# The feed-forward's operands turned by DMA transposes in a fused FNet and GEGLU kernel

## The chip, the cores and the metric

The kernel runs on one core of a Trainium2 chip. The metric is the device time in microseconds of one execution. The core has five engines that work in parallel, each through its own queue in program order: PE (TensorE, matmuls), DVE (VectorE), ACT (ScalarE), POOL (GpSimd) and SP (SyncE), which here issues every DMA. They wait for one another by semaphores. The data moves on 16 DMA engines.

## The reference

One transformer layer on x of shape 2048 x 448: h = x + FNet(layernorm(x)), then out = h + GEGLU(layernorm(h)).

```python
a = einsum("bsd,ed->bse", x, dft_hid_re);  b = einsum("bsd,ed->bse", x, dft_hid_im)
y = einsum("ts,bse->bte", dft_seq_re, a) - einsum("ts,bse->bte", dft_seq_im, b)
h = x + y                                   # x in the two lines above is layernorm(x)
g = einsum("bsd,df->bsf", n, w_gate);  u = einsum("bsd,df->bsf", n, w_up)   # n = layernorm(h)
out = h + einsum("bsf,fd->bsd", gelu(g) * u, w_down)
```

The width of the feed-forward is 1792.

## The kernel before

All matmuls take float16 operands. To keep float32 accuracy every operand is split into a high part (`hi_part`, a copy on ACT, L103) and a low part (`lo_part`, the difference, on DVE, L107 or L109), and a product is three matmuls (high x high, high x low, low x high).

The kernel has two stages. The order of the work is written out by hand: every engine runs its queue in the order in which the program names the instructions, and two tables, `early` and `after`, and later `side`, hang extra pieces of work on numbered steps.

**Stage 1, the Fourier mixing** (to about 368 us): 64 steps, `n` = 0 to 63, 16 for each block `b` of 512 outputs. Step n loads two tiles of the sequence matrix ahead (`seq_load`, SP, L366, five buffers), splits them three steps ahead (ACT L103, DVE L109) and runs 18 matmuls of 512 columns (L414) and, now and then, the remainder (L428). After a block the hidden transform follows in four pieces (`hid_mm`, L479), one every other step of the next block, and h comes out. Beside it, in steps of three, one of 14 feed-forward weight tiles is loaded, split and stored to DRAM (`Weights`; the store is L335). The blocks of h are kept in DRAM too (L490).

**Stage 2, the feed-forward** (from about 368 us): 56 steps `t`, 14 for each of four blocks `q`. Gate and up products use a Strassen scheme: a step takes 39 matmuls of 256 columns (`product`, L718) on the weight tile `gw` (loaded back by SP, L798, three buffers) and on the block's operands `hops`; from q = 1 on it takes 21 matmuls of the down projection (L662) as well.

**The operands `hops`.** A block q has two pairs j of 2 x 128 tokens (`hp[q, j]`). For each pair the kernel normalises h (`ffn_norm`, or `ffn_norm_act` for q = 2 and 3), forms the Strassen sums (`ffn_sums`), and splits them into one float16 tile `xs` of 128 tokens x 3200 columns (`ffn_hi`, `ffn_lo`). PE needs these operands with the 448 features on the partitions, so `ffn_transpose` turns the 25 column blocks of 128 of `xs` into the 25 slots of `hops[q]`, in four parts of 8, 8, 6 and 3 blocks. Each part is one tile `pt` in a single PSUM bank (`ps_tr`, tag "tr", which the pieces of `hid_mm` use as well): 8 matmuls against the identity on PE (L285), then one copy PSUM to SBUF on ACT (L287).

For q = 0 and 1 that happens in stage 1: pair j of block b splits at step n + 5 and transposes at steps n + 6, n + 7 and twice n + 9, with n = 16 (b + 1) + 1 + 6 j. For q = 2 and 3 it happens in stage 2, two blocks of steps ahead of their use: with t0 = 14 (q - 1) + 6 j the split ends in step t0 + 5, and the parts are transposed in steps t0 + 4, t0 + 5 and twice t0 + 6. `xs` has one buffer, `hops` has two.

Of the kernel before, what the change touches and what calls it, by code (L numbers as in the profile page):

```python
# [8 lines left out]
F16 = mybir.dt.float16  # L9
F32 = mybir.dt.float32  # L10
AF = mybir.ActivationFunctionType
ALU = mybir.AluOpType

P = 128
# [18 lines left out]
def kernel(  # L33
# [35 lines left out]
    nc = tc.nc  # L69
    V, A, G, PE = nc.vector, nc.scalar, nc.gpsimd, nc.tensor  # L70
# [7 lines left out]
    ps_tr = ctx.enter_context(tc.tile_pool(name="ps_tr", bufs=1, space=bass.MemoryType.PSUM))  # L78
# [3 lines left out]
    ident = const.tile([P, P], F16, name="ident")  # L82
# [195 lines left out]
    def ffn_transpose(q, j, parts):  # L278
        xs = ffn[q, j][2]
        ops = hops[q]  # L280
        for n in parts:
            s0, s1 = ((0, 8), (8, 16), (16, 22), (22, 25))[n]
            pt = ps_tr.tile([P, 8, P], F16, tag="tr", name=f"pt_{q}_{j}_{n}")
            for k in range(s0, s1):
                PE.transpose(pt[:, k - s0, :], xs[:, k * P : (k + 1) * P], ident)  # L285
            dst = ops[:, s0:s1, j * P : (j + 1) * P]
            A.activation(dst, pt[:, : s1 - s0], AF.Copy)  # L287


    for q in range(2):  # L290
# [47 lines left out]
    xt, xs, norm_x = {}, {}, {}  # L338
# [166 lines left out]
    for k, f in enumerate(reversed(range(NF))):  # L505
        n = 17 + 3 * k
# [4 lines left out]
    for b in range(NB):  # L511
        for j in range(2):
            n = (b + 1) * NT + 1 + 6 * j
            at(early, min(n - 4, N_STEPS - 3), lambda b=b, j=j: h_tile(b, j))
            if b == NB - 1:
                continue
            for g in range(2):
                at(after, (n + 2 * g, 0), lambda b=b, i=2 * j + g: hid_mm(b, i, ps_tr, "tr"))
            at(early, n + 3, lambda b=b, j=j: ffn_stats(b, j, hp[b, j]))
            at(early, n + 3, lambda b=b, j=j: h_store(b, j))  # L520
            if b < 2:
                at(early, n + 3, lambda b=b, j=j: ffn_norm(b, j, hp[b, j]))
                at(early, n + 4, lambda b=b, j=j: ffn_sums(b, j))
                at(early, n + 5, lambda b=b, j=j: ffn_split(b, j))
                for k, when in enumerate(((n + 6, 1), (n + 7, 1), (n + 9, 0), (n + 9, 1))):
                    at(after, when, lambda b=b, j=j, k=k: ffn_transpose(b, j, (k,)))
# [388 lines left out]
    for q in (2, 3):  # L915
        for j in range(2):
            t0 = (q - 1) * NF + 6 * j
            for f, k, what in (
                (0, 1, lambda q=q, j=j: ffn_norm_act(q, j, hp[q, j])),
                (1, 1, lambda q=q, j=j: ffn_sums(q, j, (0,))),  # L920
                (1, 2, lambda q=q, j=j: ffn_sums(q, j, (1,))),
                (2, 1, lambda q=q, j=j: ffn_sums(q, j, (2,))),
                (2, 1, lambda q=q, j=j: ffn_hi(q, j, (0,))),
                (2, 2, lambda q=q, j=j: ffn_sums(q, j, (3,))),
                (2, 2, lambda q=q, j=j: ffn_lo(q, j, (0,))),
                (3, 1, lambda q=q, j=j: ffn_hi(q, j, (1,))),
                (3, 2, lambda q=q, j=j: ffn_lo(q, j, (1,))),
                (4, 1, lambda q=q, j=j: ffn_lo(q, j, (2,))),
                (4, 2, lambda q=q, j=j: ffn_lo(q, j, (3,))),
                (5, 1, lambda q=q, j=j: ffn_lo(q, j, (4,))),  # L930
                (4, 4, lambda q=q, j=j: ffn_transpose(q, j, (0,))),
                (5, 4, lambda q=q, j=j: ffn_transpose(q, j, (1,))),
                (6, 4, lambda q=q, j=j: ffn_transpose(q, j, (2,))),
                (6, 5, lambda q=q, j=j: ffn_transpose(q, j, (3,))),
            ):
                at(side, (t0 + f, k), what)

    for t in range(3 * NF, N_GU):
        f = t % NF
        if f < NF - 1:  # L940
            n, k = divmod(f, 2)
# [28 lines left out]
    for t in range(N_GU):  # L970
        q, f = divmod(t, NF)
# [58 lines left out]
    for i in range(4):  # L1030
        j, g = divmod(i, 2)
# [68 lines left out]
```

## Time and profile before

| | |
|---|---|
| median of 3 runs | 741.58 us (741.35 to 742.21) |
| the profiled execution | 741.01 us, span of its instructions 738.9 us |
| granted TensorE clock | 1.00 throughout |
| busy: PE, DVE, ACT, POOL | 731.1, 500.8, 295.2, 234.1 us |
| DMA transposes | none |
| L285, 200 TensorE transposes | 16.4 us busy on PE |
| L287, 32 copies from PSUM | 26.7 us busy on ACT |
| DMA on SP's queue | 132.43 MB in 36832 packets, 51.1% of 16 engines |

A row of a group reads: line, engine, operation, output <- input, shapes, count | busy us, mean ns of one | idle us of that engine just before, and what ended it. A row of a timeline reads: start us, length us, engine, line, operation, output <- input, count, and in brackets an idle time before it. SPq is SP's queue. "us to landing" of a DMA is the time from its issue to its data being there.

### The profile page before, as it was taken

The page shows a single profiled execution, that of the slowest core. Times are in us where ns is not written, and L with a number is a line of the kernel's source. Part 1 is how long each engine was busy: PE and PEld are TensorE (multiplying, and loading weights), DVE is VectorE, ACT ScalarE, POOL GpSimd, SP SyncE. Part 2 cuts the span into 40 slices and gives each one's busy share as a digit, 9 for nine tenths or more (in the row PEclk, how much of TensorE's full clock was granted, in tenths as well). Part 3 has the DMA queues.
Part 4 walks back from the last instruction along what each step waited for, and adds up shares of the span by engine and source line. Part 5 has one row for each costly group of instructions (what it writes and reads, how often), then busy time and mean ns, then how long its engine had stood idle before and what let it go on. Part 6 is the DMA issues. An engine that isn't in the chain of part 4 may idle for free.

```text
span 738.9 us, 13783 instructions
## 1 busy us (share of the span) xinstructions
PE 731.1 (99%) x5530; PEld 511.3 (69%) x5530; DVE 500.8 (68%) x1026; ACT 295.2 (40%) x567; POOL 234.1 (32%) x274
## 2 busy tenths in 40 slices
PE   9999999999999999999999999999999999999998
PEld 5444444444444444444488889999999999999998
DVE  7888665577655776450477778687786977988730
ACT  4444613348223572221143354544545444454310
POOL 0000000000000001000058865477674866858430
PEclk9999999999999999999999999999999999999999
DMA  8666464474645567621057654345535446465411
GB/s 275 227 215 236 157 228 177 141 266 178 228 178 204 203 226 281 260 81 45 26 182 279 239 198 170 117 166 175 174 118 194 155 161 226 170 229 201 150 39 38
DMA packets 36896, 133.31 MB, mean 180 GB/s; under 512 B 3680, under 2 KB 12896, under 8 KB 36832
## 3 DMA queue, kind: packets, MB, share of 16 engines
q1 hardware_dynamic: 36832, 132.43, 51.1%
q8 instruction: 43, 0.70, 0.4%
q14 instruction: 21, 0.17, 0.1%
HBM read 112.23 MB, written 20.19 MB: 179 GB/s over the span
## 4 chain that ended last, share of the span: by engine, by line
PE 93%; DVE 3%; DMA 2%; ACT 2%; issue 0%; SPq 0%; DVEq 0%
PE acc L414 32%; PE pY L718 13%; PE acc_d L662 11%; PE y L479 9%; PE pX L718 8%; PE pZ L718 8%; PE acc L428 6%; PE pt L285 1%; PE last_Y L881 1%; PE last_X L881 1%; PE last_tr L881 1%; DMA x<-in_x_dram 1%; DMA gw<-w_dram 1%; DVE dn_w L107 1%; PE last_a L881 1%; PE last_Z L881 1%
## 5 line engine op out<-in xcount | busy, mean ns | idle before, releaser
L414 PE MATMUL acc<-ws,xs 128*128 128x512 f16 x1152 | 256.2, 379 | 0.2 <-DVE xs L107 0.2
L718 PEld LDWEIGHTS <-gw 128*128 128x128 f16 x2067 | 201.2, 98 | 23.9 <-issue 2.4
L414 PEld LDWEIGHTS <-xs 128*128 128x128 f16 x1152 | 110.6, 98 | 135.4 <-issue 6.1
L718 PE MATMUL pY<-hops,gw 128*128 128x256 f16 x901 | 123.0, 273 | 1.9 <-DVE u L728 1.7
L109 DVE SCALAR_TENSOR_TENSOR ws<-wr,ws 128x1024 f16<-128x1024 f32 (+1 forms) x66 | 78.0, 1188 | 44.1 <-ACT ws L103 44.1
L662 PE MATMUL acc_d<-wd,dn_w 128*128 128x224 f16 x882 | 105.1, 259 | 0.0
L201 POOL TENSOR_TENSOR wd_s<-wd 128x448 f32<-128x448 f32 x7 | 7.9, 1131 | 281.2 <-DMA wd<-in_w_down_dram 281.2
L662 PEld LDWEIGHTS <-dn_w 128*128 128x128 f16 x882 | 85.0, 98 | 2.9
L718 PE MATMUL pX<-hops,gw 128*128 128x256 f16 x583 | 81.0, 273 | 0.5 <-DMA gw<-w_dram 0.5
L718 PE MATMUL pZ<-hops,gw 128*128 128x256 f16 x583 | 79.2, 273 | 0.0
L785 POOL TENSOR_TENSOR hh<-hh,g 128x256 f32<-128x256 f32 x42 | 30.9, 736 | 146.1 <-DVE hh L728 127.6
L103 ACT ACTIVATE ws<-wr 128x1024 f16<-128x1024 f32 (+1 forms) x66 | 66.4, 1018 | 23.2 <-DMA wr<-in_w_seq_dram 13.3
L728 DVE SCALAR_TENSOR_TENSOR u<-pY,u 128x256 f32<-128x256 f32 x112 | 46.9, 419 | 29.5 <-ACT c L792 18.8
L479 PE MATMUL y<-wh,z 128*128 128x448 f16 x336 | 65.7, 352 | 0.0
L479 PEld LDWEIGHTS <-z 128*128 128x128 f16 x336 | 32.8, 98 | 31.6 <-issue 0.4
L107 DVE TENSOR_TENSOR dn_w<-dn_s,dn_w 128x640 f16<-128x640 f32 x42 | 53.2, 1266 | 1.4 <-ACT dn_w L103 0.9
L287 ACT ACTIVATE hops<-pt 128x1024 f16<-128x1024 f16 (+2 forms) x32 | 26.7, 834 | 67.3 <-PE pt L285 67.3
L487 DVE SCALAR_TENSOR_TENSOR hx<-y,hx 128x448 f32<-128x448 f32 x16 | 10.0, 624 | 62.4 <-PE y L479 62.4
L769 ACT ACTIVATE g<-pX 128x256 f32<-128x256 f32 x56 | 21.4, 381 | 73.3 <-PE pX L718 68.1
L756 ACT ACTIVATE u<-pX 128x256 f32<-128x256 f32 x56 | 21.4, 383 | 72.8 <-PE pX L718 72.7
L794 POOL TENSOR_TENSOR hh<-hh,c 128x256 f32<-128x256 f32 x42 | 40.9, 975 | 20.0 <-ACT c L792 20.0
L428 PE MATMUL acc<-ws,xs 128*64 128x512 f16 x384 | 44.7, 381 | 0.0
(110 smaller groups left out, 880.3 us busy)
## 6 DMA issues: line engine op xcount, KB each, us to landing
gw<-w_dram SPq DMA_DIRECT2D x53, 896.0 KB, 4.6
wr<-in_w_seq_dram SPq DMA_DIRECT2D x62, 512.0 KB, 6.2
w_dram<-gu_w SPq DMA_DIRECT2D x14, 896.0 KB, 4.7
gu_raw<-in_w_gu_dram SPq DMA_DIRECT2D x28, 384.0 KB, 5.6
wd<-in_w_down_dram SPq DMA_DIRECT2D x14, 448.0 KB, 5.3
x<-in_x_dram SPq DMA_DIRECT2D x16, 224.0 KB, 3.5
hx<-in_x_dram SPq DMA_DIRECT2D x8, 448.0 KB, 6.6
h_dram<-hx SPq DMA_DIRECT2D x8, 448.0 KB, 4.1
```

Source lines behind the costliest of these rows:

```text
L103: A.activation(dst, src, AF.Copy, scale=scale)
L107: V.tensor_sub(dst, src, hi)
L109: V.scalar_tensor_tensor(dst, src, scale, hi, op0=ALU.mult, op1=ALU.subtract)
L414: PE.matmul(acc[b, 3 * part + k], xs[c][:, lx, k * P : (k + 1) * P], seq_w(n, lw, part), start=c == 0 and m == 0, stop=c == NT - 1 and m == 2,
L428: PE.matmul(acc[b, 6][64 * part : 64 * part + 64, :], xs[c][:, lx, 3 * P :], seq_w(n, lw, part), start=c == 0 and m == 0, stop=c == NT - 1 ...
L479: PE.matmul(y[:, :D], z[b][:, lz, k, i * P : (i + 1) * P], wh[:, lw, k, :], start=k == 0 and m == 0, stop=k == 6 and m == 2,)
L662: PE.matmul(acc[k // 2][:, k % 2 * HD : (k % 2 + 1) * HD], a_of(la, a), b_of(lb, b), start=first and m == 0 and k % 2 == 0, stop=last and ...
L718: PE.matmul(ps, w[:, wl, wa + ws, :], ops[:, m + ms, :], start=first and n == 0, stop=last and n == len(terms) - 1, skip_group_check=True,)
L728: V.scalar_tensor_tensor(dst, ps, SC, other, op0=ALU.mult, op1=ALU.add)
L785: G.tensor_mul(c21, c21, self.g1)
L794: G.tensor_mul(c22, c22, self.c12)
L881: PE.matmul(banks[0][:, c * HD : (c + 1) * HD] if one else banks[c][:, 0:HD], last["h"][:, lh, f, tok], w, start=f == 0 and m == 0 and c = ...
```

## The change

In `ffn_transpose` the matmuls against the identity, the PSUM tile and the copy are replaced by one DMA per part, issued by SP, that reads the columns of `xs` and writes them transposed into the same slots of `hops`. Nothing else changes; the lines behind it move up by four.

```diff
         for n in parts:
             s0, s1 = ((0, 8), (8, 16), (16, 22), (22, 25))[n]
-            pt = ps_tr.tile([P, 8, P], F16, tag="tr", name=f"pt_{q}_{j}_{n}")
-            for k in range(s0, s1):
-                PE.transpose(pt[:, k - s0, :], xs[:, k * P : (k + 1) * P], ident)
-            dst = ops[:, s0:s1, j * P : (j + 1) * P]
-            A.activation(dst, pt[:, : s1 - s0], AF.Copy)
+            nc.sync.dma_start_transpose(ops[:, s0:s1, j * P : (j + 1) * P], xs[:, s0 * P : s1 * P])
```

SP's order in stage 1, around the first pair of block 0 (`wr` a tile of the sequence matrix, `gu_raw` and `w_dram` the feed-forward weights on their way in and out). Before:

```order
L366 DMA wr_1294<-in_w_seq_dram 128x1024
L366 DMA wr_1379<-in_w_seq_dram 128x1024
L366 DMA wr_1416<-in_w_seq_dram 128x1024
L335 DMA w_dram_165<-gu_w_1383 128x3584
L302 DMA gu_raw_1426<-in_w_gu_dram 128x768 x2
L366 DMA wr_1470<-in_w_seq_dram 128x1024
L490 DMA h_dram_147<-hx_1_1105 128x896
L366 DMA wr_1529<-in_w_seq_dram 128x1024
```

Now:

```order
L362 DMA wr_1294<-in_w_seq_dram 128x1024
L283 DMA_TRANSPOSE hops_168<-xs_0_1265 128x8x128
L362 DMA wr_1370<-in_w_seq_dram 128x1024
L283 DMA_TRANSPOSE hops_168<-xs_0_1265 128x8x128
L362 DMA wr_1398<-in_w_seq_dram 128x1024
L331 DMA w_dram_165<-gu_w_1374 128x3584
L298 DMA gu_raw_1408<-in_w_gu_dram 128x768 x2
L362 DMA wr_1452<-in_w_seq_dram 128x1024
L486 DMA h_dram_147<-hx_1_1105 128x896
L283 DMA_TRANSPOSE hops_168<-xs_0_1265 128x6x128
L283 DMA_TRANSPOSE hops_168<-xs_0_1265 128x3x128
L362 DMA wr_1500<-in_w_seq_dram 128x1024
```

The four parts stand between the weight loads, two of them in the row of three loads that had nothing between them.

SP's order in stage 2, around the second pair of block 2 (`gw` the weight tile of a step, `out_dram` a finished pair of outputs). Before:

```order
L798 DMA gw_5302<-w_dram_166 128x3584
L846 DMA out_dram<-hr_4411 128x2x448
L798 DMA gw_5406<-w_dram_167 128x3584
L798 DMA gw_5507<-w_dram_154 128x3584
L798 DMA gw_5609<-w_dram_155 128x3584
```

Now:

```order
L794 DMA gw_5157<-w_dram_166 128x3584
L283 DMA_TRANSPOSE hops_4194<-xs_1_5021 128x8x128
L842 DMA out_dram<-hr_4295 128x2x448
L794 DMA gw_5252<-w_dram_167 128x3584
L283 DMA_TRANSPOSE hops_4194<-xs_1_5021 128x8x128
L794 DMA gw_5344<-w_dram_154 128x3584
L283 DMA_TRANSPOSE hops_4194<-xs_1_5021 128x6x128
L283 DMA_TRANSPOSE hops_4194<-xs_1_5021 128x3x128
L794 DMA gw_5435<-w_dram_155 128x3584
```

Each weight load now has one or two transposes ahead of it.

ACT's order in stage 1, from the split of the first pair of block 0 on (`ws` the split of a sequence tile). Before:

```order
L103 ACTIVATE xs_0_1265<-tt_0_1228 128x192
L103 ACTIVATE ws_1296<-wr_1218 128x1024
L287 ACTIVATE hops_168<-pt_0_0_1345 128x8x128
L103 ACTIVATE ws_1296<-wr_1253 128x1024
L103 ACTIVATE gu_w_1383<-gu_raw_1102 128x512
L103 ACTIVATE gu_w_1383<-gu_raw_1102 128x256
L287 ACTIVATE hops_168<-pt_0_1_1406 128x8x128
L103 ACTIVATE ws_1418<-wr_1294 128x1024
```

Now:

```order
L103 ACTIVATE xs_0_1265<-tt_0_1228 128x192
L103 ACTIVATE ws_1296<-wr_1218 128x1024
L103 ACTIVATE ws_1296<-wr_1253 128x1024
L103 ACTIVATE gu_w_1374<-gu_raw_1102 128x512
L103 ACTIVATE gu_w_1374<-gu_raw_1102 128x256
L103 ACTIVATE ws_1400<-wr_1294 128x1024
```

The copies out of PSUM, which waited for PE, no longer stand between the splits. On PE the 8, 8, 6 and 3 transposes of a pair are taken out of the matmuls around them, whose order stays.

## The prediction

> **What bounds the kernel now.** I read the page's busy shares and its chain of waits first, then the table of stretches, then the PE timeline around the transposes.
>
> ```profile
> span 738.9 us, 13783 instructions
> PE 731.1 (99%) x5530; PEld 511.3 (69%) x5530; DVE 500.8 (68%) x1026; ACT 295.2 (40%) x567; POOL 234.1 (32%) x274
> PEclk9999999999999999999999999999999999999999
> PE 93%; DVE 3%; DMA 2%; ACT 2%; issue 0%; SPq 0%; DVEq 0%
> ...
> 0.00:60.00 60.00, 58.42 (x320) 28.68 (x320) 50.09 (x136) 27.43 (x46) 0.87 (x9) 1.00 0.71 233
> 60.00:368.00 308.00, 308.00 (x1695) 145.57 (x1695) 180.52 (x353) 115.03 (x181) 2.84 (x3) 1.00 0.52 184
> 368.00:445.00 77.00, 74.64 (x673) 65.41 (x671) 56.81 (x114) 33.36 (x71) 52.92 (x56) 1.00 0.64 222
> 445.00:704.00 259.00, 258.23 (x2517) 240.15 (x2516) 207.65 (x415) 118.37 (x269) 171.16 (x197) 1.00 0.49 170
> ```
>
> The first four rows are of the page. The others are the table of stretches: after the length come PE, PEld, DVE, ACT and POOL busy, then the granted clock and the share of the 16 DMA engines. The transposes lie in the second and the fourth stretch. There PE is busy 308.00 of 308.00 us and 258.23 of 259.00 us at full clock, and the chain of waits is 93% PE. DVE is the next engine, with 180.52 us (59%) and 207.65 us (80%). So in both stretches the time is what PE has in its queue, and a slot that leaves PE's queue leaves the span, as long as the data that took its way is there in time. ACT, at 37% and 46%, is not on the path.
>
> **What the change removes.** 200 TensorE transposes and 32 ScalarE copies:
>
> ```profile
> L285 PE MATMUL pt<-ident,xs 128*128 128x128 f16 x200 | 16.4, 219 | 0.8 <-ACT hops L287 0.8
> L287 ACT ACTIVATE hops<-pt 128x1024 f16<-128x1024 f16 (+2 forms) x32 | 26.7, 834 | 67.3 <-PE pt L285 67.3
> ```
>
> The 16.4 us busy is not yet the saving, since matmuls are pipelined and the tail of the last one of a chunk (219 ns) lies over the work that follows. The start times give the slot:
>
> ```profile
> 127.01 0.61 PE L285 MATMUL pt<-ident,xs 128*128 128x128 f16 x8
> 127.55 2.78 PE L428 MATMUL acc<-ws,xs 128*64 128x512 f16 x24
> ...
> 134.16 0.61 PE L285 MATMUL pt<-ident,xs 128*128 128x128 f16 x8
> 134.61 2.10 PE L414 MATMUL acc<-ws,xs 128*128 128x512 f16 x9
> ...
> 219.21 0.61 PE L285 MATMUL pt<-ident,xs 128*128 128x128 f16 x8
> ...
> 456.16 1.12 PE L662 MATMUL acc_d<-wd,dn_w 128*128 128x224 f16 x10
> ...
> 462.43 1.12 PE L662 MATMUL acc_d<-wd,dn_w 128*128 128x224 f16 x10
> 463.39 0.61 PE L285 MATMUL pt<-ident,xs 128*128 128x128 f16 x8
> 463.83 0.71 PE L718 MATMUL pY<-hops,gw 128*128 128x256 f16 x5
> ...
> 469.15 1.12 PE L662 MATMUL acc_d<-wd,dn_w 128*128 128x224 f16 x10
> ...
> 476.82 0.50 PE L285 MATMUL pt<-ident,xs 128*128 128x128 f16 x6
> 477.16 0.71 PE L718 MATMUL pY<-hops,gw 128*128 128x256 f16 x5
> ...
> 479.08 0.33 PE L285 MATMUL pt<-ident,xs 128*128 128x128 f16 x3 [0.39 <-ACT hops L287]
> 479.25 0.82 PE L718 MATMUL pX<-hops,gw 128*128 128x256 f16 x6
> ```
>
> A chunk of eight takes 134.61 - 134.16 = 0.45 us, or 463.83 - 463.39 = 0.44 us; one of six 0.34 us, one of three 0.17 us. The step lengths say the same from outside: a step of the feed-forward without transposes lasts 462.43 - 456.16 = 6.27 us, the next one, with a chunk of eight in it, 469.15 - 462.43 = 6.72 us. One token pair of one block needs chunks of 8, 8, 6 and 3, so 0.45 + 0.45 + 0.34 + 0.17 = 1.41 us; eight such groups (four blocks, two pairs each) are 11.3 us. To it comes the wait of PE for the single PSUM bank, 0.8 us in the row of L285. Sum: **12.1 us** off PE. The two stretches share it evenly, four groups in each.
>
> The 26.7 us of ACT copies and the 67.3 us that ACT stood waiting for PE in front of them count for nothing: ACT stays below half busy, PE hides it. If anything ACT and DVE get further ahead of PE.
>
> **What the change adds.** 32 DMA transposes on SP's queue, of 256, 192 or 96 KB (eight, six or three 128 x 128 blocks of 2 bytes). The trace has none, so I bound their landing time from plain transfers:
>
> ```profile
> q1 hardware_dynamic: 36832, 132.43, 51.1%
> ...
> gw<-w_dram SPq DMA_DIRECT2D x53, 896.0 KB, 4.6
> wr<-in_w_seq_dram SPq DMA_DIRECT2D x62, 512.0 KB, 6.2
> out_dram<-hr SPq DMA_DIRECT2D x6, 448.0 KB, 2.8
> wr<-in_w_seq_dram SPq DMA_DIRECT2D x4, 256.0 KB, 4.6
> out_dram<-hr SPq DMA_DIRECT2D x3, 224.0 KB, 2.0
> ```
>
> From below: like a plain store, between 2.0 us for 224 KB and 2.8 us for 448 KB, so 2.1 us for 256 KB. From above: a transpose works on rows of 128 elements, so 256 bytes at a time. Eight blocks are 8 x 128 = 1024 rows, 64 for each of 16 engines. The mean packet here took 0.511 x 16 x 738.9 / 36832 = 0.164 us of one engine; if each row cost that, a chunk of eight would hold all 16 engines for 64 x 0.164 = 10.5 us. I take 4.6 us, the landing of the plain 256 KB load: same bytes, same queue.
>
> The Trainium skill (VectorE: DVE Perf Modes, The three transpose paths) puts a 128 x 128 transpose at 390 ns on TensorE and at 1309 ns through the DMA crossbar, and its rules for kernel authors prefer TensorE where PSUM can take the result: that speaks against this change. By that figure, eight in a row would be an estimate of 10.5 us, the upper end above; what it would make of the time is the third rival. The skill's DMA: Bandwidth & Descriptors (Latency and other measured facts) gives a transposing DMA 261 GB/s; by it 256 KB would be an estimate of 1.0 us plus a fixed part, hidden as in the sum. No run so far shows which holds.
>
> **What hides 4.6 us.** Two things can come late: the transposed operand, and the load that stands behind the transpose on SP. In the first stage SP runs in bursts: after a store it issues three weight loads at once, and the change puts a transpose before the second and one before the third.
>
> ```profile
> 117.70 1.87 SPq L366 DMA_DIRECT2D wr<-in_w_seq_dram x3
> ...
> 137.72 1.04 ACT L103 ACTIVATE ws<-wr 128x1024 f16<-128x1024 f32 x1
> ...
> 147.52 1.05 ACT L103 ACTIVATE ws<-wr 128x1024 f16<-128x1024 f32 x1
> ```
>
> The second load of the burst is split by ACT at 137.72 us, 19 us after its issue, the third at 147.52 us, 28 us after. Landing takes 6.2 us, so some 12 and 21 us are in hand; one transpose of 4.6 us ahead of the second and two ahead of the third fit. The transposes wait for DVE's low parts, done on DVE before this burst's end; and the operands of blocks 0 and 1 are read only after 368 us.
>
> In the feed-forward the tightest place is the second pair of a block:
>
> ```profile
> 498.38 1.15 DVE L107 TENSOR_TENSOR xs<-tt,xs 128x768 f16<-128x768 f32 x1
> ...
> 509.75 0.41 DVE L107 TENSOR_TENSOR xs<-tt,xs 128x64 f16<-128x64 f32 x2
> ...
> 506.88 0.39 SPq L846 DMA_DIRECT2D out_dram<-hr x1
> 507.36 4.35 SPq L798 DMA_DIRECT2D gw<-w_dram x2
> 518.00 0.32 SPq L798 DMA_DIRECT2D gw<-w_dram x1
> ...
> 524.53 0.71 PE L718 MATMUL pX<-hops,gw 128*128 128x256 f16 x5
> ```
>
> The first transpose goes out when DVE is done at 499.5 us, the second behind the weight load of 507.36 us, at 507.7 us; the third and the fourth (DVE done at 510.2 us) behind the load of 511.4 us; and behind them stands the load of 518.00 us. PE opens the new block at 524.53 us and needs the weights of the load of 518.00 us one step later, at 524.53 + 6.27 = 530.8 us. With L for a chunk of eight, and everything one after the other on the engines, that load lands at 507.7 + L + 4.6 + 0.75 L + 0.375 L + 4.6 = 516.9 + 2.125 L. At L = 4.6 us that is 526.7 us, 4.1 us early. Trouble starts at L = 6.5 us; until then the cost is nothing. So 12.1 us stay.
>
> **Result of the sum.** The profiled execution took 741.0 us with a span of 738.9 us: 741.0 - 12.1 = 728.9 us. The median of the runs is 0.6 us above the profiled one, so 729.5 us. Changes within 0.2% (1.5 us) can't be told from none.
>
> **The rivals.**
>
> *A few transposes come late* (L between 6.5 and 7.9 us, or one place with less slack than I see). For: four groups of the feed-forward each have that deadline, and loads of 512 KB land in 6.2 us, not far from 6.5. Against: a chunk has half their bytes. At L = 7.2 us each of four groups loses 2.125 x 7.2 - 13.9 = 1.4 us, together 5.6 us: 735 us.
>
> *DVE becomes the bound in the feed-forward*, so that only the first stage gains. For: it is 80% busy there. Against: the steps without transposes run at 6.27 us with the same work on DVE. Gain 5.7 us: 736 us.
>
> *The transposes hold the DMA engines* (the other side): each 256-byte row costs what a packet costs, L = 10.5 us. In the feed-forward the load of 518.00 us lands at 539.2 us, 8.4 us late, four times: 34 us. In the first stage two groups come in 219.21 - 127.01 = 92 us; the plain transfers take 0.52 of it, 48 us, the transposes 2 x 25 blocks x 1.31 us = 66 us: 22 us too much, twice, less some 10 us in hand: 34 us. 741.6 - 12.1 + 34 + 34 = 797 us. It decides from the point where four groups lose 12.1 us: 2.125 L = 16.9, L = 8.0 us. For it: small pieces. Against it: nothing in the trace but the mean packet, and that packet has 3.6 KB. The figure of the Trainium skill named above is on its side.
>
> *The change does nothing on PE* can be excluded, since the 200 transposes are gone from PE's order.
>
> **How the numbers follow.** Forecast 0.80 (727.5 to 731.5 us; below, if an idle gap of PE goes as well, above, if a late load costs a little), a few late 0.04, DVE 0.03, DMA engines held 0.13, of which 0.03 lie near its break-even. Predicted 729.5 us. The range 727.0 to 735.0 us holds the forecast and the milder half of the two small rivals. Faster: 0.80 + 0.04 + 0.03 = 0.87; within 0.2%: 0.03; slower: 0.10.
>
> **What would show it.** PE's matmuls at L285 and ACT's copies at L287 gone; the steps that had a chunk of eight back at 6.27 us; PE still 99% busy with a span near 727 us; a row of transposes landing in 2 to 5 us; no wait of PE for hops or for gw beyond the one of before. It is wrong if transposes land above 8 us, if PE waits at L718 for DMA, or if ACT's waits for wr pass over to PE at L414.

## The result

The changed kernel takes 728.89 us (median of 4 runs, 728.56 to 729.39), the kernel before 741.47 us (740.90 to 742.21): 12.6 us less, a ratio of 0.9831 with a 95% interval of 0.9819 to 0.9844. The forecast was 729.5 us.

The page of the changed kernel, and its table of stretches (the two that hold the transposes; columns as before: PE, PEld, DVE, ACT, POOL, clock, DMA share, GB/s):

```profile
span 727.6 us, 13421 instructions
PE 719.5 (99%) x5330; PEld 499.2 (69%) x5330; DVE 500.1 (69%) x1026; ACT 271.5 (37%) x535; POOL 234.3 (32%) x274
PE 94%; DMA 3%; DVE 1%; ACT 1%; issue 0%; SPq 0%; DVEq 0%
q1 hardware_dynamic: 63456, 138.99, 58.0%
```

```profile
60.00:362.00 302.00, 302.00 (x1593) 139.57 (x1592) 180.47 (x353) 104.44 (x165) 2.84 (x3) 1.00 0.59 199
...
439.00:693.00 254.00, 254.00 (x2434) 236.26 (x2432) 208.19 (x419) 106.04 (x254) 171.98 (x198) 1.00 0.59 188
```

PE is busy for 719.5 us instead of 731.1 us, 11.6 us less, and the span is 11.3 us shorter. In both stretches PE is still busy without a gap: the 200 slots have gone and nothing has come in their place. Each stage gave about half of it: the feed-forward's first matmul starts at 365.3 us instead of 370.7 us.

The spans differ by less than the medians, 11.3 us and 12.6 us, for two reasons. The profiled execution of the kernel before, 741.01 us, is 0.5 us below the median, and that of the changed kernel, 729.39 us, is 0.5 us above it. And 0.3 us lie outside the span of the instructions: 741.01 - 738.9 = 2.1 us before, 729.39 - 727.6 = 1.8 us now.

The PE timeline shows the two steps of the feed-forward that had a chunk of eight in them (what started at 462.43 us before starts at 457.81 us now):

```profile
457.81 1.12 PE L658 MATMUL acc_d<-wd,dn_w 128*128 128x224 f16 x10
...
464.08 1.12 PE L658 MATMUL acc_d<-wd,dn_w 128*128 128x224 f16 x10
...
470.35 1.12 PE L658 MATMUL acc_d<-wd,dn_w 128*128 128x224 f16 x10
```

Both last 6.27 us; the first of them lasted 6.72 us before. The groups of PE, with what it waited for, and the two places at which it waited for `gw`:

```profile
L410 PE MATMUL acc<-ws,xs 128*128 128x512 f16 x1152 | 254.1, 379 | 0.9 <-ACT xs L103 0.6 <-DVE xs L107 0.3
L714 PE MATMUL pY<-hops,gw 128*128 128x256 f16 x901 | 123.0, 273 | 1.6 <-DVE u L724 1.5
...
L714 PE MATMUL pX<-hops,gw 128*128 128x256 f16 x583 | 81.0, 273 | 1.0 <-DMA gw<-w_dram 0.9
...
381.57 0.83 PE L714 MATMUL pX<-hops,gw 128*128 128x256 f16 x6 [0.21 <-DMA gw<-w_dram]
408.26 0.83 PE L714 MATMUL pX<-hops,gw 128*128 128x256 f16 x6 [0.73 <-DMA gw<-w_dram]
```

PE waits 0.9 us for `gw`, 0.5 us before, and never for `hops`. Both waits for `gw` lie in block 0, at 381.57 and 408.26 us, where SP's queue holds no transpose: the last of the first stage is issued at 256.3 us, the next at 455.38 us. The 0.9 us at L410 lie in the first 21 us, ahead of the first transpose (118.8 us). So no wait of PE in this trace stands at a transpose or at a load close behind one.

The transposes themselves, on SP's queue:

```profile
L283 SPq DMA_TRANSPOSE hops<-xs x32: 1216/1335/4124, 118.8 to 593.8; - x32
...
DMA to landing us min/median/max: 2.4/6.0/8.4
```

The row gives how long SP is held by one (least, median, most, in ns), the other how long its data takes to land. They are not quick: 6.0 us to landing against the 4.6 us that I took (6.2 us is the median of the sixteen chunks of eight, for which the 4.6 us stood), and 1.3 us of SP each (1.6 us for a chunk of eight, at the least 1.24 us) against 0.3 to 0.8 us for most plain loads. And they move small pieces: on SP's queue the packets grew from 36832 to 63456, by 26624, which are the 200 x 128 = 25600 rows of 256 bytes and 1024 more, 32 for each transpose. The engines' time grew from 0.511 x 16 x 738.9 = 6041 us to 0.580 x 16 x 727.6 = 6752 us, 711 us for these packets: 0.027 us for one, a sixth of the mean packet's 0.164 us. By this estimate a chunk of eight holds the 16 engines for 64 x 0.027 = 1.7 us.

### The profile page after: what moved, and what is told of

The parts are those of the page before. It is cut to its first block, busy times and chain, and to the rows that moved or that the text cites. A ratio compares the mean times of both kernels' runs of the same rounds, so it can differ in the third digit from the quotient of the medians.

```text
span 727.6 us, 13421 instructions
## 1 busy us (share of the span) xinstructions
PE 719.5 (99%) x5330; PEld 499.2 (69%) x5330; DVE 500.1 (69%) x1026; ACT 271.5 (37%) x535; POOL 234.3 (32%) x274
## 2 busy tenths in 40 slices
DMA packets 63518, 139.83 MB, mean 192 GB/s; under 512 B 30304, under 2 KB 39520, under 8 KB 63456
## 3 DMA queue, kind: packets, MB, share of 16 engines
q1 hardware_dynamic: 63456, 138.99, 58.0%
## 4 chain that ended last, share of the span: by engine, by line
PE 94%; DMA 3%; DVE 1%; ACT 1%; issue 0%; SPq 0%; DVEq 0%
PE acc L410 33%; PE pY L714 13%; PE acc_d L658 11%; PE y L475 9%; PE pX L714 9%; PE pZ L714 9%; PE acc L424 6%; DMA gw<-w_dram 2%; PE last_Y L877 1%; PE last_X L877 1%; PE last_tr L877 1%; DMA x<-in_x_dram 1%; PE last_a L877 1%; PE last_Z L877 1%; DMA wr<-in_w_seq_dram 1%; DVE ws L109 0%
## 5 line engine op out<-in xcount | busy, mean ns | idle before, releaser
L410 PE MATMUL acc<-ws,xs 128*128 128x512 f16 x1152 | 254.1, 379 | 0.9 <-ACT xs L103 0.6
L410 PEld LDWEIGHTS <-xs 128*128 128x128 f16 x1152 | 111.2, 98 | 139.6 <-issue 6.1
L475 PE MATMUL y<-wh,z 128*128 128x448 f16 x336 | 65.7, 352 | 0.0
L807 POOL TENSOR_TENSOR dn_s<-hh 128x256 f32<-128x256 f32 x42 | 43.6, 1038 | 0.0
```

The source lines that it names most:

```text
L410: PE.matmul(acc[b, 3 * part + k], xs[c][:, lx, k * P : (k + 1) * P], seq_w(n, lw, part), start=c == 0 and m == 0, stop=c == NT - 1 and m == 2,
L475: PE.matmul(y[:, :D], z[b][:, lz, k, i * P : (i + 1) * P], wh[:, lw, k, :], start=k == 0 and m == 0, stop=k == 6 and m == 2,)
L807: G.tensor_add(s[:, 0:2], t[:, 0:2], t[:, 2:4])
```

## The experiments

The theory is that the gain is the PE slots and nothing else, and that the transposes are hidden with room. The rivals are that ACT's relief gave part of the gain, and that SP or the DMA engines are near their limit.

**One stage alone.** The old path stays for the blocks of the other stage:

```diff
-            nc.sync.dma_start_transpose(...)
+            if q < 2:          # e2: q >= 2
+                nc.sync.dma_start_transpose(...)
+            else:
+                ...            # PE.transpose and the copy as before
```

> Blocks 0 and 1 (stage 1) by DMA, blocks 2 and 3 (stage 2) by TensorE and ScalarE as before. Theory (the gain is the PE slots that go): 4 groups x 1.41 us = 5.6 us off, so about 735.8 us. Rival (the gain comes from one stage, the other gives nothing): 741.5 or 729 us.

Measured: 735.04 us against 741.45 us, 6.4 us less (ratio 0.9902 to 0.9931).

> Blocks 2 and 3 by DMA, blocks 0 and 1 as before. Theory: 4 x 1.40 us and the 0.8 us for which PE waited for the PSUM bank, 6.4 us off, about 735.1 us; with the run that does stage 1 alone the two gains add up to the whole 12.6 us. Rival: as there, 729 or 741.5 us.

Measured: 734.32 us, 7.1 us less (0.9891 to 0.9924). Both stages gain. Which gains more is not shown: the intervals of either are about 1 us wide to each side. The two gains add up to 13.5 us where the whole is 12.6 us, which agree within these intervals.

**PE keeps its transposes.** Beside the DMA transposes PE does its 200 again, into a tile that nobody reads:

```diff
             nc.sync.dma_start_transpose(...)
+            pt = ps_tr.tile([P, 8, P], F16, tag="tr", ...)
+            for k in range(s0, s1):
+                PE.transpose(pt[:, k - s0, :], xs[:, k * P : (k + 1) * P], ident)
```

> All 32 DMA transposes, but PE does its 200 transposes too, into a PSUM tile that nobody reads; the ScalarE copies stay away. Theory (PE slots are all of it): 11.3 us come back, only the 0.8 us of waiting for the bank stay away, about 740.5 us. Rival (a good part comes from ACT, which no longer waits for PE and no longer copies): clearly below, 735 us or less.

Measured: 739.29 us, 2.2 us below the kernel before (0.9962 to 0.9984). The row of the transposes in this kernel:

```profile
L286 PE MATMUL pt<-ident,xs 128*128 128x128 f16 x200 | 16.4, 219 | 0.0
```

The same 16.4 us busy as before, without the 0.8 us of waiting for the bank. Of the 12.6 us, 739.29 - 728.89 = 10.4 us come back with the slots alone. That is most of it. PE's busy time comes back by 730.9 - 719.5 = 11.4 us, as the 11.3 us of the sum have it; against that PE waits 1.5 us less in this profiled execution than in that of the change, mostly in the first 21 us and for `gw` in block 0.

The other 2.2 us (1.2 to 2.8 by the interval) are more than the 0.8 us of the bank. The two profiled executions, 741.01 and 739.29 us, differ by 1.7 us: 0.8 us of the bank, 0.3 us outside the span of the instructions, and 0.2 us each of PE's busy time and of its waits at the start and for `gw`. The rest is that the profiled execution of before lies 0.4 us below the median. The trace of this run has the same 1.7 us of waiting for DVE's `u` as the one of before, so no part of the 2.2 us is seen to come from ACT by that way.

**ACT keeps its copies.** No PE transposes, but ACT copies the same columns to the same bank:

```diff
             nc.sync.dma_start_transpose(...)
+            pc = ps_tr.tile([P, 512], F32, tag="tr", ...)
+            for k in range(s0, s1, 4):
+                m = min(4, s1 - k) * P
+                A.activation(pc[:, :m], xs[:, k * P : k * P + m], AF.Copy)
```

> All 32 DMA transposes, no TensorE transposes, but ACT copies as many columns as before (from xs into the same PSUM bank, 512 columns of float32 at a time, nobody reads them): some 30 us of ACT work at the old places, not tied to PE's transposes. Theory: hidden, 729 us as with the change. Rival (ACT's 26.7 us were part of the gain): 732 to 740 us.

Measured: 730.54 us (0.9840 to 0.9869 of the kernel before), 1.6 us above the change. The copies were there:

```profile
L287 ACT ACTIVATE pc<-xs 128x512 f32<-128x512 f16 (+2 forms) x56 | 30.9, 551 | 24.1 <-DVE hx L487 21.0 <-DVE xs L107 2.2
...
L718 PE MATMUL pY<-hops,gw 128*128 128x256 f16 x901 | 122.9, 273 | 3.1 <-DVE u L728 2.9
```

So 30.9 us of ACT work at the old places are all but hidden, which excludes ACT as the source of most of the gain, though they are not hidden wholly. In this run PE waits 2.9 us for DVE's `u` at L718, 1.5 us in the changed kernel. `u` is made from an ACT copy, so work on ACT can reach PE this way. Four of the waits, 0.2 us each (at 476.0, 478.5, 564.7 and 567.2 us), come 3 to 6 us after three copies in a row on ACT; the traces of the change and of before have none in these blocks (before waits 1.7 us for `u`, all of it in block 0). So the copies can cost PE about 0.9 us at other places on ACT's queue, and the trace of the kernel before does not show that they did.

**More and smaller transposes.** The next four leave PE as in the change and load SP and the engines differently. First, most transposes are issued twice, the second into slots that are overwritten later:

```diff
             nc.sync.dma_start_transpose(ops[:, s0:s1, j * P : (j + 1) * P], ...)
+            if j == 0:
+                nc.sync.dma_start_transpose(ops[:, s0:s1, P : 2 * P], ...)
+            elif n < 2:
+                nc.sync.dma_start_transpose(ops[:, s0 + 8 : s1 + 8, P : 2 * P], ...)
```

> Most DMA transposes are issued twice: the second writes into slots of hops that are overwritten later, 41 blocks more for every 50 (4.1 MB more in all, 26 transposes more). Theory (they are hidden with room left): 729 us, within 1 us of the change, and the loads behind them land later by 1 to 3 us without PE waiting. Rival (the loads are on the edge): PE waits at L714 or L410 for DMA, 732 us or more.

(By the code it is 24 transposes and 5.4 MB more, not the 26 and 4.1 MB written there.) Measured: 729.00 us (0.9818 to 0.9852), as the change. The engines' share rises to 63.3%. PE waits 1.1 us for `gw`, in one piece at 407.81 us in block 0, where no transpose is issued. So there is room for nearly twice as much.

Then one DMA for each block instead of each part:

```diff
-            nc.sync.dma_start_transpose(ops[:, s0:s1, j * P : (j + 1) * P], xs[:, s0 * P : s1 * P])
+            for k in range(s0, s1):
+                nc.sync.dma_start_transpose(ops[:, k, j * P : (j + 1) * P], xs[:, k * P : (k + 1) * P])
```

> One DMA per 128 x 128 block, 200 instead of 32, same bytes. If SP is held for about 1.25 us by each, as it is now by a transpose of three, six or eight blocks, a group takes SP 31 us instead of 5 us: 9 x 1.25 = 11 us before the weight load behind the last two parts, which has some 8 us in hand after its landing: 3 us late in each of four groups, about 741 us. If the hold goes with the bytes (0.16 us a block), nothing changes: 729 us.

Measured: 795.64 us (792.41 to 799.16; ratio 1.0695 to 1.0769), 66.7 us above the change with the same bytes: the sign was right, the size far off. SP's queue, from its groups and from its timeline in the feed-forward:

```profile
L284 SPq DMA_TRANSPOSE hops<-xs x200: 1093/1230/2294, 119.1 to 668.3; - x100
...
DMA to landing us min/median/max: 2.2/2.5/8.7
```

```profile
472.98 10.94 SPq L284 DMA_TRANSPOSE hops<-xs  x8
484.02 0.52 SPq L795 DMA_DIRECT2D gw<-w_dram  x1
484.59 10.86 SPq L284 DMA_TRANSPOSE hops<-xs  x8
495.55 0.52 SPq L795 DMA_DIRECT2D gw<-w_dram  x1
496.11 11.31 SPq L284 DMA_TRANSPOSE hops<-xs  x9
507.52 1.00 SPq L795 DMA_DIRECT2D gw<-w_dram  x2
```

One block holds SP for 1.23 us, as long as eight blocks do at the least, and lands in 2.5 us. So the hold goes with the instruction and not with the bytes. I had counted only the nine before the last load; but each of the three loads in a row stands behind 11 us of transposes, where a step has 6.27 us, and the lateness adds up over the group. The expectation also put the first stage at nothing. There ACT waits 102.5 us for the sequence tiles in front of its splits, 28.0 us in the change, and PE 12.2 us for `z`, which ACT and DVE make in the same queues as the splits. PE's groups in this run:

```profile
L411 PE MATMUL acc<-ws,xs 128*128 128x512 f16 x1152 | 258.9, 384 | 12.8 <-DVE z L109 12.2 <-ACT xs L103 0.3 <-DVE xs L107 0.3
L715 PE MATMUL pY<-hops,gw 128*128 128x256 f16 x901 | 128.0, 279 | 5.1 <-DMA hops<-xs 3.4 <-DVE u L725 1.4
...
L715 PE MATMUL pX<-hops,gw 128*128 128x256 f16 x583 | 83.9, 279 | 28.2 <-DMA gw<-w_dram 28.2
...
L476 PE MATMUL y<-wh,z 128*128 128x448 f16 x336 | 65.7, 352 | 2.0 <-DVE hx L484 2.0
```

Against the change PE is idle longer by 12.8 - 0.9 at L411, 28.2 - 1.0 and 5.1 - 1.6 at L715 and 2.0 at L476, together 44.6 us. The rest is in the matmuls themselves, by the page of this run:

```profile
span 793.3 us, 13639 instructions
PE 740.7 (93%) x5330; PEld 507.3 (64%) x5330; DVE 502.3 (63%) x1026; ACT 271.5 (34%) x535; POOL 232.6 (29%) x274
...
PEclk9999999989999799999999999899999799899999
```

PE is busy for 740.7 us instead of 719.5 us, 21.2 us more for the same work. 44.6 + 21.2 = 65.8 us, and the span grew by 65.7 us. (On that slower PE, see the last section.)

Is it a threshold, or does every DMA cost its share? Two blocks to a DMA (the loop above in steps of two) tell it apart:

> One DMA per two blocks (the last of a pair has one): 104 transposes of 64 KB, 13 for a pair of tokens. Theory (SP is held for 1.25 us by each, whatever its size, and only what SP can't do within a step of 6.27 us is lost): 4, 4 and 5 transposes stand between two weight loads, 5.0 to 6.3 us, so they just fit: 729 to 732 us. Rival (every further DMA costs the same share, by the run with single blocks (795.6 - 728.9) / 168 = 0.40 us): 728.9 + 72 x 0.40 = 757 us.

Measured: 728.54 us (0.9812 to 0.9845): a threshold, since a cost for every DMA would have made it 757 us. SP's timeline at the same place:

```profile
460.05 0.33 SPq L796 DMA_DIRECT2D gw<-w_dram  x1
460.42 5.62 SPq L285 DMA_TRANSPOSE hops<-xs  x4
466.32 0.34 SPq L796 DMA_DIRECT2D gw<-w_dram  x1
466.76 6.30 SPq L285 DMA_TRANSPOSE hops<-xs  x5
473.16 6.02 SPq L796 DMA_DIRECT2D gw<-w_dram  x2
```

4 or 5 transposes, 5.6 to 6.3 us in these lines, fit between the loads that go out every 6.27 us. 104 transposes cost as little as 32.

At the other end, one DMA for a whole pair, at the place of the last part:

```diff
+            if n == 3:
+                nc.sync.dma_start_transpose(ops[:, :, j * P : (j + 1) * P], xs[:, :])
```

> One DMA for all 25 blocks of a pair, at the place of the last part: 8 transposes of 800 KB, which start one to two steps later than the first parts did. Theory: still hidden, 729 us; if the hold of SP were the same for every size it would be 1.3 us, if it follows the bytes beyond some size, 3 to 4 us, and neither delays a weight load that has 7.8 us in hand. Rival (the operands or the load behind them come late, since 800 KB take the engines for long): 731 us or more, with PE waiting at L715 for hops or gw.

Measured: 728.84 us (0.9818 to 0.9847), hidden as well. Its queue row:

```profile
L284 SPq DMA_TRANSPOSE hops<-xs x8: 4447/6012/7002, 140.6 to 591.7; - x8
...
DMA to landing us min/median/max: 6.3/8.3/10.4
```

25 blocks hold SP for 6.0 us (median), longer than the 3 to 4 us expected, and land in 8.3 us.

## Why the prediction was right

*What bounds the kernel.* PE, shown by the run in which PE keeps its transposes: 10.4 of the 12.6 us come back. That it is so in both stretches is shown by the two runs with one stage alone, which gain 6.4 and 7.1 us.

*The sum.* 12.1 us off PE by the slots and the bank; 12.6 us measured on the medians, 11.3 us on the two profiled spans. Taking the slot from the starts (0.45 us for eight) and not the busy time was right: the busy time of the row would have said 16.4 us. The steps went back to 6.27 us, as forecast.

*ACT counts for nothing.* Nearly: putting as many copies back costs 1.6 us, not nothing.

*The cost of a transpose.* The one term that was off. I took 4.6 us to landing between bounds of 2.1 and 10.5 us; the median is 6.0 us (6.2 us for eight blocks) and the longest 8.4 us, all inside the bounds. Two of the signs came out against the forecast: the transposes do not land in 2 to 5 us, and one lands above 8 us (8.4 us, in the first stage), which was named as a sign of being wrong. By the letter of the working, trouble would start at L = 6.5 us and break-even lie at 8.0 us, so with 6.0 us there would have been little room, and one chunk of eight in the feed-forward took 6.7 us to land. That it cost nothing comes of a margin that the working did not see: it let the transposes follow one another on the engines, each for its whole landing time, while by the estimate above a chunk of eight holds them for only 1.7 us of the 6.0. At the place that the working held tightest, SP has issued the last transposes at 507.08 us and the load behind them waits until 510.22 us for PE to free its buffer:

```profile
504.36 2.72 SPq L283 DMA_TRANSPOSE hops<-xs  x2
510.22 6.59 SPq L794 DMA_DIRECT2D gw<-w_dram  x2
```

The run with most transposes issued twice shows the room too. And the working had no term for SP itself, which a transpose holds for 1.3 us; that is the resource which gives out first when there are many, as the single blocks show.

*The rivals.* A few late: PE's wait for `gw` grew by 0.4 us only, and not at a transpose. DVE as the bound: PE stays without a gap in the feed-forward (254.00 of 254.00 us). The engines held, each row at the price of a packet: 0.027 us, not 0.164 us. The figure of the Trainium skill (VectorE: DVE Perf Modes, The three transpose paths), 1309 ns for a 128 x 128 transpose of bf16 through the DMA, is near what one such instruction holds SP for here, 1230 ns; for eight blocks in one instruction the hold is 1.6 us in the median, not eight times as much. The Trainium skill's advice (VectorE: DVE Perf Modes, Rules for kernel authors) to keep such transposes on TensorE did not pay here, where PE is busy without a gap and the slower way had the time to spare; no run here shows a kernel with another bound.

## What to carry to other kernels

When one engine is busy without a gap, work that another unit does far more slowly (here 6.0 us to landing against a slot of 0.45 us) is still a gain if its result is needed later than it takes; take the gain from the start times of the neighbours, not from the busy time. Price what takes over on every resource it uses, the issuing queue included: bytes on the DMA engines, hold on the queue, landing against the deadline. Batch it until the holds between two urgent loads fit into the time between them; past that, further batching brought nothing here.

## What the hardware showed beyond that

A DMA transpose holds its issuing queue by the instruction up to eight blocks: the medians are 1.23 us for one block, 1.24 us for two, 1.3 us for three and for six and 1.6 us for eight, of which the shortest took 1.24 us. For 25 blocks it is 6.0 us. Some take longer: the longest hold of one of eight blocks, 4.1 us, stands in a burst of weight loads in the first stage.

TensorE ran at half its clock in stretches that begin after idle times of some microseconds. In the run with single blocks, from PE's timeline and, in the last line, from a table of stretches (the granted clock, 0.50, is the third number from the end):

```profile
500.50 1.06 PE L715 MATMUL pX<-hops,gw 128*128 128x256 f16 x6 [2.55 <-DMA gw<-w_dram]
501.36 1.49 PE L715 MATMUL pY<-hops,gw 128*128 128x256 f16 x6
502.64 1.49 PE L715 MATMUL pZ<-hops,gw 128*128 128x256 f16 x6
...
512.38 1.46 PE L715 MATMUL pX<-hops,gw 128*128 128x256 f16 x6 [3.77 <-DMA gw<-w_dram]
513.63 1.49 PE L715 MATMUL pY<-hops,gw 128*128 128x256 f16 x6
...
501.00:504.00 3.00, 3.00 (x16) 2.07 (x15) 1.05 (x3) 1.62 (x4) 1.64 (x3) 0.50 0.16 33
```

Six matmuls that take 0.65 us elsewhere, from start to start, took 502.64 - 501.36 = 1.28 us soon after 2.55 us of waiting, and 1.25 us at once after 3.77 us. The length of the wait alone does not tell when the clock falls: after 4.17 us of waiting (at 612.75 us) the first six still took 0.66 us and the slow ones came behind them, and after 2.65 us (at 662.28 us) none were slow. The granted clock of that run is 0.968 in the mean, and PE was busy 21.2 us longer for the same work, so a third of the 66.7 us is not the waiting but what follows it. As an estimate, a mean of 0.968 made of full and half clock is 2 x 0.032 x 793.3 = 51 us at half clock, which would cost a busy PE 25 us. The Trainium skill (TensorE: Matmul & The Clock Gate, Why this matters for your kernels) warns of idle gaps above about 3 us between bursts of matmuls; the trace agrees at 3.77 us, and shows the half clock after 2.55 us already.
